# One constant added by VectorE, one batch's x on one queue, and three pauses changed in an attention-plus-experts kernel

## The chip, the cores and the metric

The kernel runs on one core of a Trainium2 chip. A core has TensorE (PE in the profile; its weight loads are shown as PEld), VectorE (DVE), ScalarE (ACT), GpSimd (POOL) and SyncE (SP). Each takes its own instructions in order, and they wait for one another through semaphores. SP, ACT and POOL can issue DMAs; a DMA waits in the issuing engine's order like any other instruction. The metric is the device time of one execution in microseconds, and the median of several executions is compared. Times inside a profile count from the start of the profiled span.

## What is computed

Two stages, all in float32. First an attention with a product feature map, for 4 batches, 4 heads, 1088 rows of 32 numbers:

```python
def phi(x):
    a = np.einsum('rd,bhsd->bhsr', S1, x)
    b = np.einsum('rd,bhsd->bhsr', S2, x)
    return np.einsum('bhsi,bhsj->bhsij', a, b).reshape(*x.shape[:-1], r * r)   # r = 8
q_p, k_p = (phi(q), phi(k))
kv = np.einsum('bhsf,bhsd->bhfd', k_p, v)
z = np.sum(k_p, axis=2)
num = np.einsum('bhsf,bhfd->bhsd', q_p, kv)
den = np.einsum('bhsf,bhf->bhs', q_p, z)[..., None] + 1e-06
return num / den
```

Its result, with the heads side by side, is x of 4352 rows by 128. Then a layer of 8 experts whose weights come from 8 rounds of Sinkhorn scaling:

```python
logits = x @ w_gate
logits = logits - logits.max()
P = np.exp(logits)                         # 4352 x 8
for _ in range(8):
    P /= P.sum(1, keepdims=True) + 1e-09
    P /= P.sum(0, keepdims=True) + 1e-09
    P *= N / E
for e in range(E):
    h = np.maximum(x @ w1[e], 0.0)         # 1024 wide
    out += P[:, e:e + 1] * (h @ w2[e])
```

## The kernel before

**The stages.** x is kept transposed in SBUF as `xT` (128 features by 4352 rows). Batch 0 is made by a path of its own (`query_products`, `multiply`, `fractions`, `divide`). Batches 1 to 3 go through `attention(b)`. Then `routing()` makes the logits, runs the Sinkhorn rounds and writes the expert weights P to DRAM (`pT`). Expert work, the large part of PE's products, starts early on rows of x that exist already, without weights (the first eight entries of `groups`, all for experts 0 and 1), and goes on with weighted x (`xe`) once P is there, from about 185 us on. The experts' second products use Strassen-like schemes: `two`/`seven` replace eight block products by seven, `four`/`twenty` do so on two levels; the sums that these need are made by VectorE (line 943 before 190 us, line 990 after).

**What sets the order.** The order on PE, DVE and ACT is the program's own, within `manual_schedule`. Expert work is a generator, `steps()`. Each of its steps issues one pair of first products (`first`, line 926), their move out of PSUM by ACT (line 930), sums on DVE that are due, and second products (`second`, line 1111) of eight steps before. `attention` and `routing` are generators too: they issue their own instructions and then yield a number, and `fill(n)` issues expert steps worth about that number before they go on. One step is worth 0.87 with the 416-row tiles that are in use around the logits. `fill` carries what it owes or has overdrawn into the next pause:

```python
    def fill(n):
        owed[0] += n
        while owed[0] > 0.25:
            owed[0] -= next(work)
```

So a `yield` sets how much expert work stands between two steps of attention or routing, on PE, DVE and ACT at once. Combining sums of a finished group (lines 750 and 753) wait in two lists, `soon` and `later`, and are issued one at a time by the steps.

**Banks.** PSUM has eight banks. Four of them (`bank()`, tiles named `a`) serve in turn for everything that is not the expert layer's long accumulation: the first products of each step, the outputs of `tops`, the three blocks of logits, and the column sums of routing. A bank can be taken again when whoever reads it has been issued, and the writer then waits until that reader is done. The other four (tiles `s`) hold the second products.

**One batch of attention.** `keys_sums` makes kv and z of a batch, `keys_kept` puts them into `kvs`, whose column D holds z. The queries come in three parts of 96 columns in each quarter (`third`). For part c, `times(b, c)` makes the products of the feature map on DVE; `tops(b, c)` multiplies them on PE by `kvs` into one bank (12 products, line 474), which gives numerators and, in column D, denominators; two more products of `ones` with the constant `eps` (1e-6 / 128 everywhere, line 478) add 1e-6 to the denominators in the same accumulation. `over(b, c)` then takes the reciprocal (line 487), multiplies (line 489) and transposes (line 493) on DVE into the tile `xt`.

**From xt to xT.** `take_over(b, lo, hi, queue)` carries columns lo to hi of `xt` to `xT`: one DMA writes them to a buffer `xd` in DRAM (line 498), four DMAs read them back in another arrangement (line 500). The reads wait for the write to land. For batches 1 and 2 all 288 columns (`W9`) go at once on POOL's queue. Batch 3 goes in two pieces: columns 0 to 192 on POOL's queue after `over(3, 1)`, and 192 to 288 on SP's queue after `over(3, 2)`.

**Logits and routing.** `logits(c)` makes a block of logits for the four batches side by side, batch 3 last, in 32-column tiles (line 508); each block takes one of the four banks `a`. `logits_turned` transposes each block on DVE (line 517) and so frees its bank. Then come the maximum (lines 593 to 600), the exponential on ACT, and the eight rounds: row sums, reciprocal, product and partial column sums on DVE (lines 608 to 614), the column sums on PE (line 618), and reciprocal and product on DVE (lines 621 and 624). At the end SP writes `pT` (line 630).

Of the kernel before, what the change touches and what calls it, by code (L numbers as in the profile page):

```python
# [10 lines left out]
F32 = mybir.dt.float32  # L11
# [39 lines left out]
def kernel(  # L51
# [12 lines left out]
    nc = tc.nc  # L64
    P = nc.NUM_PARTITIONS
    B, H, S, D = q.shape
# [77 lines left out]
    for i in range(2):  # L144
        kvs.append(consts.tile([P, 2, 2, D + 1], F32, name=f"kvs{i}"))
        nc.gpsimd.memset(kvs[i], 0.0)

    eps = consts.tile([P, 3, H], F32, name="eps")
    nc.gpsimd.memset(eps, 1e-6 / P)

    v_slots = []
    for i in range(2):
# [314 lines left out]
    def tops(b, c):  # L467

        pn = bank()[:, 0:3 * H * (D + 1)].rearrange("p (t h d) -> p t h d", t=3, h=H)
        ph = third(phs[b % 2], c)  # L470
        for t in range(3):
            for i in range(2):
                for s in range(2):
                    nc.tensor.matmul(pn[64 * s:64 * (s + 1), t, 2 * i:2 * i + 2].rearrange("p h d -> p (h d)"),  # L474
                                     ph[:, i, s, 64 * t:64 * (t + 1)], kvs[b % 2][:, i].rearrange("p h d -> p (h d)"),
                                     start=(t == 0 and i == 0), stop=False, tile_position=(0, 64 * s))
        for s in range(2):
            nc.tensor.matmul(pn[64 * s:64 * (s + 1), :, :, D], ones[:, 0:64], eps, start=False, stop=True,
                             tile_position=(0, 64 * s))
        queries[b, c] = pn  # L480

    turned = {}
# [1 line left out]
    def over(b, c):  # L484
        pn = queries.pop((b, c))
        rc = wk.tile([P, 16], F32, tag="rc", name="rc")[:, 0:12].rearrange("p (t h) -> p t h", h=H)
        nc.vector.reciprocal(rc, pn[:, :, :, D])
        xs = wk.tile([P, 512], F32, tag="rd", name="rd")[:, 0:384].rearrange("p (h t d) -> p h t d", h=H, t=3)
        nc.vector.tensor_tensor(xs.rearrange("p h t d -> p t h d"), pn[:, :, :, 0:D],
                                rc.unsqueeze(3).to_broadcast([P, 3, H, D]), op=Alu.mult)  # L490
        if c == 0:
            turned[b] = wk.tile([P, H, W9], F32, tag="xt", name="xt", bufs=1)
        nc.vector.transpose(out=turned[b][:, :, 96 * c:96 * (c + 1)].rearrange("p h (t s) -> p h t s", t=3), in_=xs)
# [25 lines left out]
    def attention(b):  # L519


        follows = b + 1 < B
        keys_sums(b)
        times(b, 0)
        yield 2.2 if b == 1 else 2
        keys_kept(b)
        times(b, 1)
        tops(b, 0)
        if b == 1:
            transpose_q(2)  # L530
        yield 1.4
        times(b, 2)
        over(b, 0)
        tops(b, 1)
        if b == 1:
            queries_ab(2)
            repeat_a(2)
        if follows:
            repeat_b(b + 1)
        yield 1.4  # L540
        over(b, 1)
        if b + 1 == B:
            take_over(b, 0, 192, nc.gpsimd)
        yield 1.4
        tops(b, 2)
        if follows:
            transpose_k(b + 1)
        if b + 2 < B:
            load_k(b + 2)
            load_v(b + 2)  # L550
        yield 1.4
        over(b, 2)
        if b + 1 < B:
            take_over(b, 0, W9, nc.gpsimd)
        else:
            take_over(b, 192, W9, nc.sync)
        if follows:
            yield 0.7
            keys_ab(b + 1)
            yield 0.7  # L560
            if b == 1:
                transpose_q(3)
            keys_products(b + 1, 0)
            yield 1.4
            keys_products(b + 1, 1)
            if b == 1:
                queries_ab(3)
                repeat_a(3)
            yield 1.4
            keys_products(b + 1, 2)  # L570
            yield 1.4
# [10 lines left out]

    def routing():

        yield 5
        for c in range(len(chunks)):
            logits(c)
        yield 1
        for c in range(len(chunks)):
            logits_turned()  # L590
        lg = lgp[:, :, 0:E]
        mx = sk.tile([P, 1], F32, tag="mx", name="mx")
        nc.vector.tensor_reduce(out=mx, in_=lg, axis=AX.XY, op=Alu.max)
        yield 3
        pm = bank()[:, 0:P]
        for s in range(2):
            nc.tensor.matmul(pm[64 * s:64 * (s + 1)], mx.to_broadcast([P, 64]), ident, start=True, stop=True,
                             tile_position=(0, 64 * s))
        nc.vector.reduce_max(mx, pm, axis=AX.X)
        nc.vector.tensor_scalar(mx, mx, -1.0, 64 * math.log(2.0), op0=Alu.mult, op1=Alu.add)  # L600
        pw = p2s[0]
        nc.scalar.activation(out=pw[:, :, 0:E], in_=lg, func=Act.Exp, bias=mx[:, 0:1])

        step = 1.5 * 2.0 ** (23 - 149 + 64)
        nc.vector.tensor_scalar(pw[:, :, 0:E], pw[:, :, 0:E], step, step, op0=Alu.add, op1=Alu.subtract)
        for it in range(ITERS):
            rs = sk.tile([P, SA], F32, tag="rs", name="rs")
            nc.vector.reduce_sum(rs, pw, axis=AX.X)  # L608
            nc.vector.reciprocal(rs, rs)
            p1 = p1s[it % 2]  # L610
            nc.vector.scalar_tensor_tensor(p1[:, 0:SA], rs.unsqueeze(2).to_broadcast([P, SA, E]), UP,
                                           pw[:, :, 0:E], op0=Alu.mult, op1=Alu.mult)
            cs = sk.tile([P, E], F32, tag="cs", name="cs")
            nc.vector.reduce_sum(cs, p1.rearrange("p g e -> p e g"), axis=AX.X)  # L614
            yield 4.25
            pc = bank()[:, 0:E]
            for s in range(2):
                nc.tensor.matmul(pc[64 * s:64 * (s + 1)], ones[:, 0:64], cs, start=True, stop=True,
                                 tile_position=(0, 64 * s))
            cr = sk.tile([P, E], F32, tag="cr", name="cr")  # L620
            nc.vector.reciprocal(cr, pc)
            last = it == ITERS - 1
            pw = lgp if last else p2s[(it + 1) % 2]
            nc.vector.scalar_tensor_tensor(pw[:, :, 0:E], cr.unsqueeze(1).to_broadcast([P, SA, E]),
                                           float(N) / E * (1.0 if last else UP), p1[:, 0:SA],
                                           op0=Alu.mult, op1=Alu.mult)

        nc.vector.transpose(out=lgT.rearrange("p a s -> p (a s)"), in_=lgp.rearrange("p a e -> p (a e)"))
        for b in (1, 0, 2, 3):
            nc.sync.dma_start(out=pT[:, b * S:(b + 1) * S],  # L630
                                                  in_=lgT[32 * b:32 * b + E].rearrange("p a s -> p (a s)"))
# [653 lines left out]
```

## Time and profile before

| | |
|---|---|
| median of 4 runs | 920.72 us (920.26 to 921.01) |
| the profiled execution | 920.52 us |
| its span | 918.7 us |
| busy: PE, DVE, ACT, POOL | 911.7, 688.5, 421.2, 213.2 us |
| granted TensorE clock | 1.00 |
| products with `ones` and `eps` (L478) | 36 records, 35.6 to 97.8 us |
| products of `tops` (L474) | 216 records, 34.9 to 97.7 us |
| logits (L508) | 24 records, 107.0 to 108.6 us |
| DMA reads of batch 3's last piece on SP | issued 102.7 to 104.0 us, 1.9 us to landing |

A row of the timeline gives the start in us, the busy time in us, the engine, the source line, the operation, what it writes and reads, the number of records that were merged, and in brackets how long the engine sat idle before and what released it. A float32 product leaves two records. Records of PE overlap, because a product's record lasts until its last result is out while the next has begun; where PE is the subject, the distance of two starts is the time that a product costs. The chain that ended last follows the work back from the last instruction; an engine's share of it says how much of the span was spent waiting for that engine.

### The profile page before, as it was taken

Reading aid. Unit: us, or ns where it says so; the run is one execution under the profiler, and the core shown is the slowest. Engines: PE = TensorE matmul, PEld = TensorE weight load, DVE = VectorE, ACT = ScalarE, POOL = GpSimd, SP = SyncE. Lnnn points to the kernel's source line nnn. Section 1 sums busy time; section 2 is a strip of 40 time slices with the busy share of each in tenths; the row PEclk is TensorE's granted clock in tenths of the full one; section 3 lists DMA queues with packets and bytes.
Section 4 is the critical chain, followed back from the end, with each engine's and each line's share of the span. In section 5 each row is a group of like instructions: output and inputs, shape, how many; then the busy total and the mean of one; then the engine's idle time right before and its main releaser. Section 6 shows DMA issues by size and latency. Waiting matters only on the chain.

```text
span 918.7 us, 18917 instructions
## 1 busy us (share of the span) xinstructions
PE 911.7 (99%) x7450; PEld 601.5 (65%) x7450; DVE 688.5 (75%) x1173; ACT 421.2 (46%) x915; POOL 213.2 (23%) x220
## 2 busy tenths in 40 slices
PE   9999999999999999999999999999999999999997
PEld 6877544466666666666666666666666666668665
DVE  7678699888877798756985666956567986668665
ACT  3355465554444454444544444544445444446443
POOL 5121100175545422200210011110100353221120
PEclk9999999999999999999999999999999999999999
DMA  9994100213554535534364343463335556452650
GB/s 250 301 280 165 54 1 1 70 64 124 157 152 132 176 129 163 176 110 148 114 181 139 114 146 109 128 194 123 136 116 168 153 149 195 158 169 93 177 151 13
DMA packets 91305, 128.15 MB, mean 139 GB/s; under 512 B 25392, under 2 KB 69504, under 8 KB 86480
## 3 DMA queue, kind: packets, MB, share of 16 engines
q1 hardware_dynamic: 88384, 121.42, 42.3%
q0 software_dynamic: 1600, 5.36, 2.0%
q8 instruction: 58, 0.95, 0.4%
q10 hardware_dynamic: 1232, 0.16, 0.1%
q14 instruction: 31, 0.25, 0.1%
HBM read 107.88 MB, written 19.05 MB: 138 GB/s over the span
## 4 chain that ended last, share of the span: by engine, by line
PE 97%; DVE 1%; DMA 1%; issue 0%; ACT 0%; SPq 0%; DVEq 0%
PE a L926 57%; PE s L1111 37%; PE a L352 1%; PE a L474 1%; DMA kx<-in_k_dram 1%; PE a L319 0%; DVE hb L943 0%; PE s L381 0%; PE a L438 0%; PE s L404 0%; PE a L508 0%; PE a L387 0%; PE a L404 0%; DVE cs L614 0%; DVE rs L608 0%
## 5 line engine op out<-in xcount | busy, mean ns | idle before, releaser
L926 PE MATMUL a<-xe,w 128*64 128x256 f32 (+1 forms) x2560 | 692.0, 470 | 0.0
L926 PEld LDWEIGHTS a<-xe,w 128*64 128x64 f32 x2560 | 320.6, 137 | 112.6 <-issue 1.6
L1111 PE MATMUL s<-hb,ws 128*64 128x256 f32 (+3 forms) x1312 | 331.6, 395 | 0.2 <-DVE hb L943 0.2
L1111 PE MATMUL s<-hx,ws 128*64 128x256 f32 x1280 | 306.3, 379 | 0.0
L930 ACT ACTIVATE hb<-a 128x256 f32<-128x256 f32 (+4 forms) x408 | 195.0, 480 | 242.2 <-PE a L926 210.2
L930 ACT ACTIVATE hx<-a 128x256 f32<-128x256 f32 (+1 forms) x360 | 167.0, 464 | 213.4 <-PE a L926 193.0
L990 DVE TENSOR_TENSOR hb<-hb 128x512 f32<-128x512 f32 (+1 forms) x204 | 140.6, 699 | 98.3 <-ACT hb L930 94.2
L1111 PEld LDWEIGHTS s<-hb,ws 128*64 128x64 f32 x1312 | 158.5, 137 | 70.1 <-issue 14.1
L990 DVE TENSOR_TENSOR hx<-hx 128x512 f32<-128x512 f32 (+1 forms) x204 | 155.4, 772 | 59.8 <-ACT hx L930 54.4
L690 POOL TENSOR_TENSOR xe<-xT,xe 128x768 f32<-128x768 f32 (+2 forms) x41 | 84.6, 2064 | 479.6 <-DMA xe<-pT 371.8
L1111 PEld LDWEIGHTS s<-hx,ws 128*64 128x64 f32 x1280 | 154.6, 137 | 57.3
L1111 PE MATMUL s<-hb,w 128*64 128x256 f32 (+3 forms) x536 | 134.7, 408 | 0.0
L926 PE MATMUL a<-xT,w 128*64 128x416 f32 (+3 forms) x512 | 120.5, 462 | 0.0
L1111 PE MATMUL s<-hx,w 128*64 128x256 f32 x384 | 95.6, 379 | 0.0
L1111 PEld LDWEIGHTS s<-hb,w 128*64 128x64 f32 x536 | 61.1, 137 | 22.9 <-issue 6.9
L943 DVE TENSOR_TENSOR hb<-hb 128x416 f32<-128x416 f32 (+7 forms) x84 | 60.3, 718 | 19.4 <-ACT hb L930 15.0
L926 PEld LDWEIGHTS a<-xT,w 128*64 128x64 f32 x512 | 50.7, 137 | 23.8 <-issue 15.1
L242 POOL TENSOR_TENSOR ws<-w 128x256 f32<-128x256 f32 (+1 forms) x70 | 62.1, 920 | 6.3 <-DMA w<-in_moe_w_dram 6.3
L943 DVE TENSOR_TENSOR hx<-hx 128x256 f32<-128x256 f32 (+1 forms) x65 | 39.0, 604 | 23.6 <-ACT hx L930 22.5
L1111 PEld LDWEIGHTS s<-hx,w 128*64 128x64 f32 x384 | 46.2, 137 | 11.6 <-DVE hx L943 0.3
L990 DVE TENSOR_TENSOR pqg<-hb 128x512 f32<-128x512 f32 x68 | 44.2, 690 | 0.0
L990 DVE TENSOR_TENSOR pqg<-hx 128x512 f32<-128x512 f32 x68 | 34.7, 549 | 0.0
(184 smaller groups left out, 486.5 us busy)
## 6 DMA issues: line engine op xcount, KB each, us to landing
w<-in_moe_w_dram SPq DMA_DIRECT2D x82, 512.0 KB, 5.6
ws<-ws SPq DMA_DIRECT2D x34, 1024.0 KB, 5.0
xe<-pT SPq DMA_DIRECT2D x34, 384.0 KB, 3.9
ws<-ws SPq DMA_DIRECT2D x12, 512.0 KB, 4.0
ph<-qa SPq DMA_DIRECT2D x12, 288.0 KB, 5.2
rb<-qb SPq DMA_DIRECT2D x3, 1152.0 KB, 7.6
pb<-pT SPq DMA_DIRECT2D x6, 384.0 KB, 7.6
kx<-in_k_dram SPq DMA_DIRECT2D x4, 544.0 KB, 5.1
```

The source lines that it names most:

```text
L242: tc.keep_in_program_order(nc.gpsimd.tensor_tensor(ws[:, c:c + len(ns)], blocks(x), blocks(y), op=Alu.subtract if off else Alu.add))
L352: nc.tensor.matmul(pv[64 * s:64 * (s + 1), i], kp[0:n, H * t + h].rearrange("p i j -> p (i j)"), vx[0:n, slots[h], t, :], start=(t == 0 an ...
L474: nc.tensor.matmul(pn[64 * s:64 * (s + 1), t, 2 * i:2 * i + 2].rearrange("p h d -> p (h d)"), ph[:, i, s, 64 * t:64 * (t + 1)], kvs[b % 2] ...
L690: tc.keep_in_program_order(nc.gpsimd.tensor_tensor(out, x, pb, op=Alu.mult))
L926: nc.tensor.matmul(ph[sl], loaded_w[j][0][:, P * f + H2 * s:P * f + H2 * (s + 1)], sources[j][:, lo:hi], start=True, stop=True, tile_posit ...
L930: nc.scalar.activation(out=out, in_=ph, func=Act.Relu)
L943: nc.vector.tensor_tensor(out, a, b, op=Alu.subtract)
L990: nc.vector.tensor_tensor(out if not isinstance(out, tuple) else places(*out), places(*a), places(*b) if isinstance(b, tuple) else b, op=A ...
L1111: nc.tensor.matmul(sums[g][i][H2 * s:H2 * (s + 1), n * place:n * (place + 1)], w, x, start=c == 1, stop=c == per, tile_position=(0, H2 * s))
```

## The change

The constant `eps` and the products with it go; `tops` ends its accumulation with its own last product. `over` adds 1e-6 to the denominators on DVE before the reciprocal. The first piece of batch 3 goes to SP's queue instead of POOL's, which puts it ahead of the second piece on the same queue. In `attention`, the pause between `tops(b, 2)` and `over(b, 2)` is 0.6 instead of 1.4 for the last batch. In `routing`, the pause ahead of the logits is 6 instead of 5.

```diff
-    eps = consts.tile([P, 3, H], F32, name="eps")
-    nc.gpsimd.memset(eps, 1e-6 / P)
-
@@ def tops(b, c):
                     nc.tensor.matmul(pn[64 * s:64 * (s + 1), t, 2 * i:2 * i + 2].rearrange("p h d -> p (h d)"),
                                      ph[:, i, s, 64 * t:64 * (t + 1)], kvs[b % 2][:, i].rearrange("p h d -> p (h d)"),
-                                     start=(t == 0 and i == 0), stop=False, tile_position=(0, 64 * s))
-        for s in range(2):
-            nc.tensor.matmul(pn[64 * s:64 * (s + 1), :, :, D], ones[:, 0:64], eps, start=False, stop=True,
-                             tile_position=(0, 64 * s))
+                                     start=(t == 0 and i == 0), stop=(t == 2 and i == 1), tile_position=(0, 64 * s))
         queries[b, c] = pn
@@ def over(b, c):
-        nc.vector.reciprocal(rc, pn[:, :, :, D])
+        nc.vector.tensor_scalar_add(rc, pn[:, :, :, D], 1e-6)
+        nc.vector.reciprocal(rc, rc)
@@ def attention(b):
         over(b, 1)
         if b + 1 == B:
-            take_over(b, 0, 192, nc.gpsimd)
+            take_over(b, 0, 192, nc.sync)
         yield 1.4
         tops(b, 2)
...
-        yield 1.4
+        yield 1.4 if follows else 0.6
         over(b, 2)
@@ def routing():
-        yield 5
+        yield 6
         for c in range(len(chunks)):
             logits(c)
         yield 1
```

## The prediction

> **What bounds the kernel now.** I read the page's busy shares and the chain that ended last first, then the timelines of TensorE (PE) around the six edits, then the timelines of the queues (SP, POOL), VectorE (DVE) and ScalarE (ACT) beside them.
>
> ```profile
> PE 911.7 (99%) x7450; PEld 601.5 (65%) x7450; DVE 688.5 (75%) x1173; ACT 421.2 (46%) x915; POOL 213.2 (23%) x220
> ...
> PE 97%; DVE 1%; DMA 1%; issue 0%; ACT 0%; SPq 0%; DVEq 0%
> ```
>
> PE is busy 911.7 of 918.7 us and 97% of the chain. So a change counts by what PE no longer executes and by the waits PE gets or loses; the other engines count only where PE waits for them. All edits act before 200 us; behind that PE meets the same work in the same order.
>
> ```profile
> 37.54 0.90 PE L474 MATMUL a<-kvs,ph 128*64 128x66 f32 x24
> 38.24 0.27 PE L478 MATMUL a<-eps,ones 128*64 128x12 f32 x4
> 38.33 0.56 PE L438 MATMUL a<-qT,wdq 128*64 128x192 f32 x4
> ```
>
> Read starts, not durations, since matmuls overlap: the removed products hold PE from 38.24 to 38.33, 0.09 us.
>
> ```profile
> 95.65 0.73 POOL L498 DMA_DIRECT2D xd<-xt  x1 [12.11 <-DVE xt L493]
> 99.20 2.19 POOL L500 DMA_DIRECT2D xT<-xd  x4 [2.82 <-DMA xd<-xt]
> ```
> ```profile
> 99.47 0.57 SPq L498 DMA_DIRECT2D xd<-xt  x1
> 102.71 1.74 SPq L500 DMA_DIRECT2D xT<-xd  x4
> ```
> ```profile
> 107.01 2.04 PE L508 MATMUL a<-xT,wg 128*32 128x512 f32 x24
> 108.98 0.92 PE L926 MATMUL a<-xT,w 128*64 128x416 f32 x4
> 109.72 0.87 PE L1111 MATMUL s<-hb,w 128*64 128x416 f32 x4
> 110.42 0.87 PE L926 MATMUL a<-xT,w 128*64 128x416 f32 x4
> ```
>
> Batch 3's x reaches xT by two write-and-read-back trips, which overlap because two queues issue them. The last of SP's four reads starts at 104.0 and lands 1.9 us later, at 105.9; the logits (L508) start at 107.01, 1.1 us behind it. So this transfer is hidden, by 1.1 us and no more.
>
> **The change, part by part.**
>
> *Products of ones (L478).* Nine `tops` lose 0.09 us each on PE: -0.8 us, six ninths of it by 87 us, all by 98 us. Bounds: 0 where PE waits right behind, 0.9 at 0.10 us each as the chain counts them. The memset of `eps` runs on POOL in the first microseconds, off the chain: 0.
>
> *Addition on DVE.* Nine additions of 128x12; nearest row: the same operation at L417 takes 0.17 us, and neighbours on DVE start 0.03 us after one another's end, so 0.2 us each (0.17 to 0.25). Behind each stand `over`'s own product and transpose and the next sums for PE. DVE works without a pause from 64.5 to 84.8 us. There the first of the two sums of the row at 69.50 is over at 69.9 and PE uses it at 70.84; that of the row at 74.24 is over at 74.6 and used at 75.57: 0.9 us of cover. One addition lies ahead of the first and two ahead of the second since DVE's last pause, and PE comes 0.2 to 0.3 us sooner: at most 0.7 of the 0.9 goes. I take 0; the upper end, all nine in PE's way, is 1.8.
>
> *Batch 3 on SP.* Nine instructions stay what they are, but SP works in order: write of 192 columns, wait for its landing, four reads, then the write of the last 96, wait, four reads. The diff's words and the order part here: the last third's write, which SP issues at 99.47 now, stands behind five new DMAs. DVE:
>
> ```profile
> 94.78 0.58 DVE L493 STREAM_TRANSPOSE xt<-rd 128x384 f32<-128x384 f32 x1
> ...
> 98.87 0.58 DVE L493 STREAM_TRANSPOSE xt<-rd 128x384 f32<-128x384 f32 x1
> ```
>
> The first two thirds are ready at 95.36; DVE's chain starts 0.5 us earlier (six `tops`) and carries two additions: 95.3. Write until reads may issue: SP's row for half the bytes takes 102.71 - 99.47 = 3.24, POOL's for the same bytes 99.20 - 95.65 = 3.55, POOL's other two trips, of half as many bytes again, 4.04 and 5.26:
>
> ```profile
> 47.08 0.59 POOL L498 DMA_DIRECT2D xd<-xt  x1 [4.51 <-DVE xt L493]
> ...
> 52.34 2.20 POOL L500 DMA_DIRECT2D xT<-xd  x4 [2.55 <-DMA xd<-xt]
> ...
> 77.32 0.59 POOL L498 DMA_DIRECT2D xd<-xt  x1 [12.52 <-DVE xt L493]
> 81.36 2.19 POOL L500 DMA_DIRECT2D xT<-xd  x4 [3.44 <-DMA xd<-xt]
> ```
>
> I take 3.55 (same bytes): 98.85. Four reads issue in 1.74: SP is free at 100.6, though the last third is ready at 99.6. Its trip is SP's own row: 3.24 to 103.85, last read 1.3 later, landing 1.9 later: **107.05 in place of 105.9**. PE, 0.8 us ahead, would start the logits at 106.2, and the fourth logits product waits for that landing: it starts at 107.15 where it now starts at 107.03. So the 0.8 us are spent here, and 0.1 more: +0.95 us, bounds 0.4 (write at 3.24 and half the additions' delay) to 3.5 (5.26, then 4.04). Behind the waiting product on PE stand all the other logits and expert products; SP's next DMA after them issues at 165.4, so nothing on SP is late. POOL, which loses its five DMAs, next works at 181.0.
>
> The Trainium skill, "DMA: Bandwidth & Descriptors", section "Issuing engines are not separate DMA queues", says that issuing from several engines saves only the sequencer's issue time. The rows above show that issue time (1.74 us), and it is what the edit gives up. The same page's "Specifications" puts the first byte at about 1 us from POOL and 0.6 from SP; by that the first write would be 0.4 us quicker and the sum 0.4 lower, which no row here shows.
>
> *The pauses (0.6 for 1.4, 6 for 5).* In the built programs PE's order is the same up to and through the logits: the sum of the pauses grows by 0.2 units, less than a step, and no expert work comes ahead of them. What moves is behind: one more step stands between the logits and their transposes (L517), and two of the eight column sums (L618, the fourth and seventh) stand one step later. Both have a price.
>
> Four PSUM banks serve `first`, logits and column sums in turn. The logits hold three until L517 has read them. Before, one step follows on the fourth bank; in the changed program three in a row take that bank, each waiting until ACT has emptied it.
>
> ```profile
> 110.00 0.52 ACT L930 ACTIVATE hb<-a 128x416 f32<-128x416 f32 x1 [1.36 <-PE a L926]
> 110.64 0.51 ACT L766 COPY m<-s 128x416 f32<-128x416 f32 x1
> 111.40 0.52 ACT L930 ACTIVATE hb<-a 128x416 f32<-128x416 f32 x1 [0.25 <-PE a L926]
> ```
>
> A step of 108.98 is emptied at 110.52; the next may start at 110.57, not 110.42: 0.15; the second at the pace of 1.40 loses 1.59 - 1.40 = 0.19. Sum +0.35 (0 to 1.35, the latter if a copy of 0.5 us stands ahead of ACT twice). L517 moves behind the sum of L753 that waits for the copy at 110.64; it is then over at 113.4, in time for the maximum at 115.3.
>
> ```profile
> 145.75 1.21 DVE L943 TENSOR_TENSOR hb<-hb 128x416 f32<-128x416 f32 x2
> ...
> 166.25 1.14 DVE L943 TENSOR_TENSOR hb<-hb 128x384 f32<-128x384 f32 x2
> ```
>
> In routing PE waits three times for sums that stand behind a Sinkhorn iteration on DVE: 0.20 us at 140.53, 0.16 at 146.39, 0.34 at 166.85. The fourth iteration now comes behind the sums of 145.75: -0.16. The seventh's column sums move from 161.84 by one step of 1.3 and end at 163.4; DVE takes them at 163.57: 0 (up to +0.3, since the chain runs through DVE there). Taken: -0.15.
>
> **Sum**, against the profiled execution (920.52, span 918.7): -0.8 + 0 + 0.95 + 0.35 - 0.15 = +0.35, so 920.9. The median of the runs is 0.2 above that execution: **921.1**.
>
> **Rivals.**
> A. *The transfer stays hidden*, landing by 106.2: -0.8 + 0.35 - 0.15 = -0.6, 920.1. For: 1.1 us of cover now. Against: the five DMAs ahead on SP cost 1.2 and PE comes 0.8 sooner.
> B. *DVE becomes the bound in attention*: up to 1.8 us over the forecast, 922.9 at the end, about 921.9 with half. For: DVE's unbroken stretch. Against: 0.9 us of cover where it is least.
> C. *Slower*: SP's two trips take POOL's slower rows, 5.26 and 4.04; the landing comes at 109.6, 2.5 us later than forecast: 923.6. It passes 0.2% (1.8 us, about what a measurement of this kernel can tell from no change) once the landing is behind 108.5. For: two trips in a row on one queue, the worst rows are of this very operation. Against: those had other traffic beside them, and here there is none.
> D. *More than meant*: the transfer is hidden, no bank wait, and all three routing waits go: -0.8 - 0.7 = -1.5, 919.2; past -0.2% (918.9) only with 0.3 us that I can't place.
>
> **How the numbers follow.** Forecast 0.5, A 0.18, B 0.09 (a third of it slow), C 0.14, D 0.09 (two thirds past the bound). Faster 0.06, same 0.77, slower 0.17. The range runs from D's 919.2 to 923.2, towards C; the forecast's own is 920.1 (lower ends of its terms) to 922.5 (a copy ahead of both bank waits, and 0.45 on the seventh iteration and its stall).
>
> **What would show it.** Right: no L478 rows; SP's second write some 1.2 us later than 99.47; PE idle or a semaphore wait of about 1 us ahead of L508's fourth product; three steps after the logits about 1.6 us apart; the idle at 146.39 gone, that at 166.85 still there. Wrong: logits at 106.2 without a wait; PE waiting for DVE sums between 60 and 85 us; the logits further back in PE's order.

## The result, and the profile after

The changed kernel takes 922.02 us (median of 34 executions, 920.34 to 923.89), the kernel before 920.29 (54 executions, 919.4 to 921.28): ratio 1.0017, 95% interval 1.0013 to 1.0022. It is slower by 1.7 us, inside the 0.2% that the forecast of 921.1 called the same, but its single executions spread over 3.5 us where those of before spread over 1.9. The profiled execution took 922.71 us, with a span of 920.9.

Busy shares and the chain that ended last, of the changed kernel:

```profile
PE 912.6 (99%) x7414; PEld 600.7 (65%) x7414; DVE 685.8 (74%) x1182; ACT 421.5 (46%) x915; POOL 211.2 (23%) x214
...
PE 92%; DMA 3%; DVE 3%; issue 0%; SPq 0%; ACT 0%; DVEq 0%
```

36 matmuls fewer, 9 VectorE instructions more. (The diff changes two pauses; the title counts three.) PE had 97% of the chain and has 92%: DMA and VectorE have stepped in. Where they do, PE's timeline shows (start, duration, engine, line, operation; in brackets the idle time ahead and what ended it). The line numbers are smaller by 3 to 6 than before; L471 is `tops`, L435 `queries_ab`, L921 and L1106 the expert products, L503 the logits, L484 the product in `over`.

```profile
37.13 0.90 PE L471 MATMUL a<-kvs,ph 128*64 128x66 f32 x24
37.84 0.85 PE L435 MATMUL a<-qT,wdq 128*64 128x192 f32 x8
38.85 0.55 PE L435 MATMUL a<-qT,wdq 128*64 128x192 f32 x4 [0.16 <-DVE rd L484]
...
39.71 0.60 PE L1106 MATMUL s<-hb,w 128*64 128x256 f32 x4
40.53 0.71 PE L921 MATMUL a<-xT,w 128*64 128x288 f32 x4 [0.22 <-DVE rd L484]
...
77.36 0.92 PE L921 MATMUL a<-xT,w 128*64 128x416 f32 x4 [0.31 <-DVE rd L484]
...
107.19 1.06 PE L503 MATMUL a<-xT,wg 128*32 128x512 f32 x6
108.82 1.99 PE L503 MATMUL a<-xT,wg 128*32 128x512 f32 x18 [0.58 <-issue]
110.74 0.92 PE L921 MATMUL a<-xT,w 128*64 128x416 f32 x4
...
112.34 0.92 PE L921 MATMUL a<-xT,w 128*64 128x416 f32 x4
...
113.93 0.92 PE L921 MATMUL a<-xT,w 128*64 128x416 f32 x4
...
168.81 0.54 PE L1106 MATMUL s<-hb,ws 128*64 128x384 f32 x1 [0.18 <-DVE hb L938]
```

The products of ones are gone: L435 follows L471. But L435 now comes in two pieces, and three times PE waits for `rd`, the tile that L484 writes. PE doesn't read `rd`. It waits because L484 is the last reader of the PSUM bank that `tops` filled, and PE's next product wants that bank. VectorE's timeline at the first two of these places, and at the end of batch 3:

```profile
37.78 0.16 DVE L481 TENSOR_SCALAR rc<-a 128x12 f32<-128x12 f32 x1
37.98 0.23 DVE L482 RECIPROCAL rc<-rc 128x12 f32<-128x12 f32 x1
38.24 0.56 DVE L484 TENSOR_TENSOR rd<-a,rc 128x384 f32<-128x384 f32 x1
...
39.83 0.56 DVE L484 TENSOR_TENSOR rd<-a,rc 128x384 f32<-128x384 f32 x1
...
95.70 0.58 DVE L488 STREAM_TRANSPOSE xt<-rd 128x384 f32<-128x384 f32 x1
...
99.96 0.58 DVE L488 STREAM_TRANSPOSE xt<-rd 128x384 f32<-128x384 f32 x1
```

L484 ends at 38.80 and 40.39; PE goes on at 38.85 and 40.53. The same places before (VectorE, then PE's step at the second):

```profile
37.92 0.56 DVE L489 TENSOR_TENSOR rd<-a,rc 128x384 f32<-128x384 f32 x1
...
39.31 0.56 DVE L489 TENSOR_TENSOR rd<-a,rc 128x384 f32<-128x384 f32 x1
...
40.25 0.69 PE L926 MATMUL a<-xT,w 128*64 128x288 f32 x4
```

There the product ended at 38.48 and 39.87, and PE, which came later, did not have to wait. Each addition takes 0.16 us, or 0.20 with the gap behind it (37.78 to 37.98), as estimated, but it stands between PE's bank and its release.

Near 38.8 us the addition is not alone. Just ahead of it VectorE stood for the load of q, which it did not do before:

```profile
35.71 1.31 DVE L299 STREAM_TRANSPOSE qT<-qx 128x1088 f32<-128x1088 f32 x1 [0.32 <-DMA qx<-in_q_dram]
```

Without these 0.32 us the product would have ended at 38.48, and PE's ninth product of L435 was due at 38.51 (eight twelfths of 1.00 us behind 37.84): almost no wait. Four more profiles below, with the additions on VectorE in this order (add_alone, add_queue, add_pauses and more_cover), have such a stand, 0.20 to 0.50 us; before, queue_alone, pauses_alone and add_on_act have none. It comes ahead of the first addition, so the addition does not cause it; what does was not tried. The waits near 40.5 and 77.4 us do not rest on it. Without it and the wait that it makes, VectorE and PE would both reach the first of them about 0.3 us sooner. Ahead of the other no such load stands, and VectorE's product ends 0.89 us later than before (77.30 for 76.41), 0.6 of it for three additions.

SP's queue of the changed kernel, with the trips of batch 3's x:

```profile
96.31 0.57 SPq L493 DMA_DIRECT2D xd<-xt  x1
99.29 1.74 SPq L495 DMA_DIRECT2D xT<-xd  x4
101.12 1.64 SPq L493 DMA_DIRECT2D xd<-xt  x1
104.68 1.73 SPq L495 DMA_DIRECT2D xT<-xd  x4
```

The last third's write starts 1.65 us later than before's 99.47. Three of the four logits products of the first chunk run from 107.19; the fourth, which needs batch 3, starts at 108.82, 1.6 us late. The profile puts the last 0.58 us of this to "issue"; that it is the transfer follows from the last read, which starts at 105.98 and lands 2.8 us later, at 108.8. Its later blocks then run without the other three column groups beside them, so the lateness of the start is the price: the block ends about 1.6 us later than it would have.

The starts of equal pieces of work on PE, from both timelines, give the account:

| work | before | after | difference |
|---|---|---|---|
| L1111/L1106, ahead of all edits | 25.80 | 25.37 | -0.43 |
| L1111/L1106 ahead of 40 | 39.82 | 39.71 | -0.11 |
| the next L1111/L1106 | 40.73 | 41.04 | +0.31 |
| L1111/L1106 near 72.7 | 72.72 | 72.66 | -0.06 |
| L1111/L1106 near 78 | 77.58 | 78.10 | +0.52 |
| logits | 107.01 | 107.19 | +0.18 |
| first step behind the logits | 108.98 | 110.74 | +1.76 |
| matmul of the maximum | 115.32 | 117.48 | +2.16 |
| L1111/L1106 near 168 | 167.88 | 169.84 | +1.96 |
| span | 918.7 | 920.9 | +2.2 |

The -0.43 at the top is no work of the change: the same row starts at 25.35 with the queue alone edited, and at 25.84 with the pauses alone. From there to the logits this execution loses 0.6 us where the forecast had it gain 0.8; at the logits 1.6 more; behind them 0.4, of which 0.2 come back, and 0.2 towards the end.

### The profile page after: what moved, and what is told of

Same layout as the page of the kernel before. It is cut to its first block, busy times and chain, and to the rows that moved or that the text cites. A ratio compares the mean times of both kernels' runs of the same rounds, so it can differ in the third digit from the quotient of the medians.

```text
span 920.9 us, 18857 instructions
## 1 busy us (share of the span) xinstructions
PE 912.6 (99%) x7414; PEld 600.7 (65%) x7414; DVE 685.8 (74%) x1182; ACT 421.5 (46%) x915; POOL 211.2 (23%) x214
## 4 chain that ended last, share of the span: by engine, by line
PE 92%; DMA 3%; DVE 3%; issue 0%; SPq 0%; ACT 0%; DVEq 0%
PE a L921 55%; PE s L1106 36%; DMA qx<-in_q_dram 1%; DMA kx<-in_k_dram 1%; DMA qb<-qab 1%; DVE hb L938 1%; PE a L349 1%; DMA v<-in_v_dram 1%; PE a L471 0%; PE a L503 0%; DVE rd L484 0%; DVE ph L462 0%; DVE cs L609 0%; DVE qT L299 0%; SPq L170 0%
## 5 line engine op out<-in xcount | busy, mean ns | idle before, releaser
L921 PE MATMUL a<-xe,w 128*64 128x256 f32 (+1 forms) x2560 | 692.0, 470 | 0.0
L921 PEld LDWEIGHTS a<-xe,w 128*64 128x64 f32 x2560 | 320.5, 137 | 112.6 <-issue 1.6
L1106 PE MATMUL s<-hb,ws 128*64 128x256 f32 (+3 forms) x1312 | 331.5, 395 | 0.2 <-DVE hb L938 0.2
L1106 PE MATMUL s<-hx,ws 128*64 128x256 f32 x1280 | 306.3, 379 | 0.0
L985 DVE TENSOR_TENSOR hb<-hb 128x512 f32<-128x512 f32 (+1 forms) x204 | 135.0, 671 | 102.3 <-ACT hb L925 98.5
L1106 PEld LDWEIGHTS s<-hb,ws 128*64 128x64 f32 x1312 | 158.6, 137 | 69.3 <-issue 14.5
L685 POOL TENSOR_TENSOR xe<-xT,xe 128x768 f32<-128x768 f32 (+2 forms) x41 | 86.1, 2100 | 498.9 <-DMA xe<-pT 359.2
L1106 PEld LDWEIGHTS s<-hx,ws 128*64 128x64 f32 x1280 | 154.5, 137 | 57.3
L1106 PE MATMUL s<-hb,w 128*64 128x256 f32 (+3 forms) x536 | 134.7, 408 | 0.0
L921 PE MATMUL a<-xT,w 128*64 128x416 f32 (+3 forms) x512 | 120.0, 462 | 0.5 <-DVE rd L484 0.5
L1106 PE MATMUL s<-hx,w 128*64 128x256 f32 x384 | 95.7, 380 | 0.0
L1106 PEld LDWEIGHTS s<-hb,w 128*64 128x64 f32 x536 | 61.1, 137 | 22.7 <-issue 6.7
L921 PEld LDWEIGHTS a<-xT,w 128*64 128x64 f32 x512 | 50.2, 137 | 25.8 <-issue 15.1
L938 DVE TENSOR_TENSOR hx<-hx 128x256 f32<-128x256 f32 (+1 forms) x65 | 36.9, 572 | 26.4 <-ACT hx L925 25.3
L1106 PEld LDWEIGHTS s<-hx,w 128*64 128x64 f32 x384 | 46.1, 137 | 11.8 <-DVE hx L938 0.6
```

What stands on the lines that cost most here:

```text
L685: tc.keep_in_program_order(nc.gpsimd.tensor_tensor(out, x, pb, op=Alu.mult))
L921: nc.tensor.matmul(ph[sl], loaded_w[j][0][:, P * f + H2 * s:P * f + H2 * (s + 1)], sources[j][:, lo:hi], start=True, stop=True, tile_posit ...
L938: nc.vector.tensor_tensor(out, a, b, op=Alu.subtract)
L985: nc.vector.tensor_tensor(out if not isinstance(out, tuple) else places(*out), places(*a), places(*b) if isinstance(b, tuple) else b, op=A ...
L1106: nc.tensor.matmul(sums[g][i][H2 * s:H2 * (s + 1), n * place:n * (place + 1)], w, x, start=c == 1, stop=c == per, tile_position=(0, H2 * s))
```

## The experiments

Medians and ratios to the kernel before, run on the same chip (before: 920.37, 920.51 and 920.23 us in the three groups):

| kernel | us, lowest to highest | ratio, 95% interval |
|---|---|---|
| add_alone | 920.61, 919.26 to 922.19 | 1.0001, 0.9992 to 1.0010 |
| queue_alone | 920.53, 919.53 to 921.01 | 1.0002, 0.9993 to 1.0010 |
| pauses_alone | 920.35, 920.13 to 920.88 | 1.0001, 0.9993 to 1.0010 |
| add_on_act | 920.01, 919.38 to 921.11 | 0.9996, 0.9987 to 1.0005 |
| add_queue | 922.29, 921.08 to 923.03 | 1.0019, 1.0010 to 1.0028 |
| add_pauses | 922.10, 919.94 to 923.74 | 1.0019, 1.0009 to 1.0029 |
| add_moved_product | 941.97, 940.6 to 945.49 | 1.0244, 1.0224 to 1.0263 |
| act_moved_product | 942.30, 940.23 to 943.02 | 1.0239, 1.0225 to 1.0253 |
| more_cover | 920.68, 919.19 to 923.51 | 1.0006, 0.9998 to 1.0015 |
| add_earlier_over | 922.40, 922.2 to 923.27 | 1.0024, 1.0015 to 1.0033 |
| act_earlier_over | 921.55, 919.84 to 922.53 | 1.0008, 0.9999 to 1.0017 |
| act_earlier_more_cover | 921.25, 919.78 to 924.05 | 1.0012, 1.0003 to 1.0022 |

The ratio is taken over the executions and is not quite that of the two medians. An interval is 0.8 us to either side, so the medians alone part only the larger effects; the waits in the profiles have to carry the rest.

### The three parts, one at a time, and the addition on another engine

**add_alone**

```diff
-        nc.tensor.matmul(..., ones[:, 0:64], eps, start=False, stop=True, ...)   # both, and eps
-        nc.vector.reciprocal(rc, pn[:, :, :, D])
+        nc.vector.tensor_scalar_add(rc, pn[:, :, :, D], 1e-6)
+        nc.vector.reciprocal(rc, rc)
```

> Only the addition on VectorE in place of the products of ones; queue and pauses as before. Theory (banks): the nine products leave PE (-0.8 us), but each addition puts off the product of `over` that frees the PSUM bank, and PE waits for that bank (idle put down to DVE, tile rd) near 38.8, 40.5 and 77.4 us, 0.3 to 0.6 us each, 0.7 to 1.3 us in all; batch 3's transfer stays hidden. Time -0.1 to +0.5 us against before. Rival (the forecast's term of 0 for the additions): no such waits, -0.8 us.

PE's timeline of add_alone:

```profile
38.65 0.55 PE L435 MATMUL a<-qT,wdq 128*64 128x192 f32 x4 [0.30 <-DVE rd L484]
...
40.34 0.71 PE L921 MATMUL a<-xT,w 128*64 128x288 f32 x4 [0.22 <-DVE rd L484]
...
77.16 0.92 PE L921 MATMUL a<-xT,w 128*64 128x416 f32 x4 [0.31 <-DVE rd L484]
...
106.99 1.06 PE L503 MATMUL a<-xT,wg 128*32 128x512 f32 x6
108.71 1.99 PE L503 MATMUL a<-xT,wg 128*32 128x512 f32 x18 [0.67 <-DMA xT<-xd]
```

The three waits for `rd` are here with the additions alone (queue_alone, below, whose PE is as early, has none). So is what I had not expected: the wait for batch 3's x at the logits, 1.7 us in this execution, although POOL's queue still takes the first piece. The eleven executions fall into two groups, six from 919.26 to 920.61 and five from 921.61 to 922.19; the profiled one, 922.19, is the slowest of all. The median of 920.61 lies where it was expected, but says little about either group.

**queue_alone** and **pauses_alone**

```diff
-            take_over(b, 0, 192, nc.gpsimd)
+            take_over(b, 0, 192, nc.sync)
```

> Only batch 3's first piece moved to SP's queue; products of ones and pauses as before. Theory: x ready at 95.36 as before, then SP's own legs as the changed kernel's profile has them (2.98 to the reads, 1.83 for the reads, 3.56 to the next reads, 1.3 to the last read) put the last read at 105.1 and its last landing 1.9 to 2.7 us later, 107.0 to 107.8; PE needs it at 107.03: a wait of 0 to 0.8 us ahead of the fourth logits product, +0 to +0.8 us, and more spread between executions than before. Rival (the queue is hidden; the changed kernel's wait comes from VectorE being late): no wait, within 0.2 us of before.

```diff
-        yield 1.4                          # ahead of the last over
+        yield 1.4 if follows else 0.6
...
-        yield 5                            # ahead of the logits
+        yield 6
```

> Only the two pauses changed (0.6 for 1.4, 6 for 5). Theory: two waits for the one free bank behind the logits, 0.15 and 0.19 us, and the idle of 0.16 us near 146.4 gone: +0.2 us (0 to 0.5). Rival (the pauses are worth nothing, or gain): 0 to -0.2 us.

SP's queue and PE's logits in queue_alone (timeline):

```profile
95.05 0.57 SPq L498 DMA_DIRECT2D xd<-xt  x1
99.02 1.74 SPq L500 DMA_DIRECT2D xT<-xd  x4
100.85 0.55 SPq L498 DMA_DIRECT2D xd<-xt  x1
103.36 1.73 SPq L500 DMA_DIRECT2D xT<-xd  x4
...
106.68 2.04 PE L508 MATMUL a<-xT,wg 128*32 128x512 f32 x24
```

All 24 logits products run in one piece of 2.04 us, as before: the whole of batch 3 on one queue is hidden when nothing else is changed. The rival for this run holds, in this profile and in the median (+0.16 us). Neither this kernel nor pauses_alone has a wait for `rd`. In pauses_alone the first three steps behind the logits start at 108.95, 110.54 and 112.14, 1.59 and 1.60 apart where before has 1.44 and 1.40: the two waits for the single bank, 0.35 us together. The idle near 146 is gone (146.25, 146.60 and 146.95 in step, where before jumps from 145.88 to 146.39). The net, 0.1 us, cannot be told from none in the median.

**add_on_act**

```diff
-        nc.vector.reciprocal(rc, pn[:, :, :, D])
+        nc.scalar.add(rc, pn[:, :, :, D], 1e-6)      # products of ones and eps gone
+        nc.vector.reciprocal(rc, rc)
```

> The products of ones replaced by an addition on ScalarE (ACT) instead of VectorE; queue and pauses as before. VectorE then executes what it did before. Theory (banks): no wait on DVE's rd between 34 and 80 us, all of the 0.8 us is kept: -0.8 us. Rival 1 (PE loses the 0.8 us anyway, at whatever it waits for next): 0, with waits in the same places as in add_alone. Rival 2 (nine instructions of about 0.2 us delay ACT's emptying of PE's banks): above -0.4 us, with PE waits put down to ACT between 34 and 100 us.

The waits near 38.8, 40.5 and 77.4 us are not in its profile, which ties the last two to the additions on VectorE (VectorE did not stand for the load of q here either). But one new wait is, at 67.59 us (waits of PE's weight loads between 60 and 75 us: engine, line, what it waited for, total, times, longest):

```profile
PEld a L921 <- DVE rd L484: 0.6, 1, 0.6
```

By the two timelines PE is 1.02 us ahead of before two steps earlier (64.63 for 65.65), 0.83 at the row just ahead (66.81 for 67.64) and 0.48 at the wait's end (67.59 for 68.07); VectorE's product ends at 67.54. So part of what PE wins is given back at the next bank, even where VectorE has nothing more to do. The median is 0.36 us under before and the interval holds both 0 and the expected -0.8; "keeps the whole" is not shown, and neither is a gain.

### What the three parts do together

**add_queue** (the changed kernel with the old pauses) and **add_pauses** (the changed kernel with POOL's queue):

```diff
-        yield 1.4 if follows else 0.6      # add_queue: back to 1.4, and 6 back to 5
-            take_over(b, 0, 192, nc.sync)  # add_pauses: back to nc.gpsimd
```

> The changed kernel with the old pauses (addition on VectorE and SP's queue for all of batch 3). Theory (the two parts add up at the logits): x is ready about 0.9 us later against PE because of the additions, and SP then starts the last third behind its own reads, so the fourth logits product waits 1 to 2 us; with the waits for banks near 39, 40.5 and 77 us, +1.3 to +1.8 us against before. Rival (the pauses carry the loss): +0.2 us or less.

> The changed kernel with batch 3's first piece back on POOL's queue (addition on VectorE and new pauses). Theory: the last third's write starts about 0.7 us earlier than in the changed kernel, but still 0.9 us later than before, and the fourth logits product waits 0 to 1.5 us depending on how long the write's leg takes; with the two bank waits behind the logits, +0.2 to +1.0 us against before, and between 0.7 and 1.3 us under the changed kernel. Rival (the queue is worth nothing): as the changed kernel, +1.7 us.

Both lose what the changed kernel loses, 1.8 and 1.6 us by their medians. For add_queue that is as expected, for add_pauses it is not: taking the queue edit back gains nothing. By the medians, though, the addition alone is at 1.0001 and either of the other two edits on top of it at 1.0019, while each of these alone is at 1.0001 or 1.0002. So by the medians the loss belongs to the addition in combination with another edit (the intervals of 1.0001 and 1.0019 only just touch); by itself the addition was seen to wait at the logits in one execution, its slowest. What the kernels with the addition on VectorE share there is read best from one number, the time from the end of VectorE's last transpose of batch 3 (the last third is then ready to be written) to the start of the logits on PE, the cover of that transfer:

| kernel | last transpose ends | logits start | cover | SP's last write to its first read | last read landed, behind the transpose | lateness of the fourth product |
|---|---|---|---|---|---|---|
| before | 99.45 | 107.01 | 7.56 | 3.24 | 6.5 | 0 |
| pauses_alone | 99.42 | 106.98 | 7.56 | 2.66 | 6.0 | 0 |
| queue_alone | 99.11 | 106.68 | 7.57 | 2.51 | 7.5 | 0 |
| add_on_act | 99.25 | 106.29 | 7.04 | 3.76 | 7.0 | 0 |
| add_alone | 100.35 | 106.99 | 6.64 | 4.52 | 8.3 | 1.7 |
| changed kernel | 100.54 | 107.19 | 6.65 | 3.56 | 8.2 | 1.6 |
| add_queue | 101.51 | 108.15 | 6.64 | 3.45 | 7.6 | 1.1 |
| add_pauses | 100.90 | 107.54 | 6.64 | 4.63 | 8.4 | 1.8 |

(The lateness is the start of the fourth product less the start of the logits; where the timeline has the block as one group, it is what the group takes over 2.04. The landing is the start of SP's last read and its time to landing.) The cover is the same to 0.01 us for the three kernels without a change to the products, and again for the four with the addition on VectorE: 0.92 us less. The parts can be read from VectorE's last wait ahead of the transpose (for ACT; 87.57 before, 88.10 in the changed kernel): from there PE takes 19.44 and 19.09 us to the logits, VectorE 11.88 and 12.44 to the end of the transpose. So 0.35 goes with the products (PE comes sooner) and 0.56 with three additions (VectorE comes later).

But the cover is only a part of the lateness. The transfer itself differs: the last read landed 6.0 to 7.5 us behind the transpose in the hidden rows and 7.6 to 8.4 in the late ones. With a transfer like before's, 6.5 us, a cover of 6.64 would have hidden it too; and the transfers of the late rows, to the fourth product 7.7 to 8.5 us, would have been 0.2 to 0.9 late at 7.56 as well. The lost cover thus accounts for 0.92 us of each lateness, the longer transfer for the rest. In the changed kernel its write starts 0.58 us behind the transpose, behind SP's own reads, and its last read lands 2.8 us after its start, for 1.9 before. Whether one of the edits lengthens the transfer, or these single profiles met long ones, is open.

### More cover

**more_cover** is the changed kernel with 0.6 undone:

```diff
-        yield 1.4 if follows else 0.6
+        yield 1.4
```

> The changed kernel with the pause of 1.4 put back ahead of the last `over` (0.6 undone, 6 kept). In the built program one whole step more of expert products (1.40 us) then stands ahead of the logits, and the three steps on one bank behind them are gone. Theory (the loss at the logits is lost cover): x has 1.4 us more until PE needs it, the wait ahead of the fourth logits product goes from 0.7-1.6 us to 0-0.3, the two bank waits behind the logits go; the waits for banks near 39, 40.5 and 77 us stay: 0 to +0.6 us against before, 1.1 to 1.7 us under the changed kernel, and less spread. Rival (the transfer itself is slowed by the queue, or the loss is elsewhere): +1.3 us or more against before.

Timeline of more_cover, PE:

```profile
40.28 0.71 PE L921 MATMUL a<-xT,w 128*64 128x288 f32 x4 [0.22 <-DVE rd L484]
...
77.11 0.92 PE L921 MATMUL a<-xT,w 128*64 128x416 f32 x4 [0.32 <-DVE rd L484]
...
108.34 2.04 PE L503 MATMUL a<-xT,wg 128*32 128x512 f32 x24
110.31 0.92 PE L921 MATMUL a<-xT,w 128*64 128x416 f32 x4
...
281.10 1.08 PE L921 MATMUL a<-xe,w 128*64 128x512 f32 x4 [0.49 <-POOL xe L685]
```

With 1.4 us of expert products more ahead of the logits the cover is 8.04 us and there is no wait. In this profile that proves little: its last read landed 6.4 us behind the transpose, which 6.64 would have hidden too. The next step behind the logits, at 111.76, is 1.45 behind the first, so the bank waits there are gone. Two of the three waits in attention stay. The median falls to 920.68 us, 1.3 under the changed kernel's (the intervals of the two ratios overlap a little). That was the expected size, and it speaks against the rival that the queue itself is the loss. The spread did not fall as expected (919.19 to 923.51), and the profiled execution, the second slowest at 922.08, has new waits: SP's write of the routing's result starts at 172.87 (before 172.15), a product of POOL with that result (L685) at 238.46 (before 235.87), and PE waits for two such products, 0.49 us at 281.10 and 0.51 at 300.77. Most of that lag arises on POOL behind the routing, so that the longer pause causes it is not shown.

### Freeing the banks sooner

**add_moved_product** and **act_moved_product** were meant to free the banks 0.9 us sooner by moving one product of VectorE:

```diff
-        times(b, 2)                        # was ahead of over(b, 0)
         over(b, 0)
...
         over(b, 1)
+        times(b, 2)
```

> As add_alone (addition on VectorE, queue and pauses as before), with one more edit: VectorE's product of the last third's features (`times(b, 2)`, 0.9 us) moved from ahead of `over(b, 0)` to behind `over(b, 1)`. The additions stay, but the banks come free 0.9 us sooner. Theory (banks): the waits for DVE's rd near 38.8 and 40.5 us vanish, that near 77.4 us stays (0.3 to 0.6); batch 3's first two thirds are ready sooner; -0.5 to 0 us against before. Rival (the loss comes from the additions' load on VectorE as a whole, not from where the banks come free): as add_alone, +0.2 us with waits of the same size.

> As add_on_act (addition on ScalarE, queue and pauses as before), with `times(b, 2)` moved behind `over(b, 1)`. Theory (banks): the wait of 0.6 us for DVE's rd near 67.6 us, where PE gave back what it had gained, vanishes too; all of the 0.8 us is kept at the logits: -0.8 us against before. Rival (PE is held by another wait as soon as this one goes): -0.4 us or less, as add_on_act.

The load of the next batch's factors (`repeat_b`) writes the tile that this product reads, and it now stood ahead of it: the product took the next batch's factors, so these two kernels compute something else, and `tops` waited for that load:

```profile
PE a L471 <- DVE ph L462: 19.4, 2, 17.0
```

(PE's waits of add_moved_product between 30 and 110 us.) Their 20 us say nothing about banks. In the next three the load moves along.

**add_earlier_over**, **act_earlier_over** and **act_earlier_more_cover**

```diff
-        times(b, 2)
         over(b, 0)
...
-        if follows:
-            repeat_b(b + 1)
         yield 1.4
         over(b, 1)
+        times(b, 2)
+        if follows:
+            repeat_b(b + 1)
```

(on add_alone; on add_on_act; on add_on_act with the pause of 6.)

> As add_alone (addition on VectorE, queue and pauses as before), with VectorE's product of the last third's features (`times(b, 2)`, 0.9 us) moved from ahead of `over(b, 0)` to behind `over(b, 1)`, and the load of the next batch's factors (`repeat_b`) moved with it. The additions stay, but the banks come free 0.9 us sooner. Theory (banks): the waits for DVE's rd near 38.8 and 40.5 us vanish, that near 77.4 us stays (0.3 to 0.6); the last third of batch 3 is not sooner, so a wait of 0 to 1.7 us ahead of the fourth logits product stays: -0.6 to +0.8 us against before. Rival (the loss in attention comes from the additions' load on VectorE as a whole): waits of the same size as in add_alone.

> As add_on_act (addition on ScalarE, queue and pauses as before), with `times(b, 2)` and `repeat_b` moved behind `over(b, 1)`. Theory (banks): the wait of 0.6 us for DVE's rd near 67.6 us, where PE gave back what it had gained, vanishes; PE is 0.8 us ahead at the logits, with 0.5 us less cover than before, so most of the executions keep the whole: -0.9 to -0.4 us against before. Rival (PE is held by another wait as soon as this one goes): as add_on_act, -0.4 us.

> As act_earlier_over, with the routing's pause of 6 for 5 (that of 1.4 ahead of the last `over` as before), so that one whole step more stands ahead of the logits. Theory (cover): never a wait ahead of the fourth logits product, the whole 0.8 us is kept in every execution, and the spread is that of before or less: -0.9 to -0.6 us against before; a routing wait may grow, since the routing starts 1.4 us later against PE (0 to +0.4). Rival (the cover was enough already, and the later routing costs): slower than act_earlier_over by 0.2 us or more.

PE's timeline of add_earlier_over:

```profile
37.71 1.17 PE L435 MATMUL a<-qT,wdq 128*64 128x192 f32 x12
38.68 0.68 PE L921 MATMUL a<-xT,w 128*64 128x288 f32 x4
...
39.60 0.68 PE L921 MATMUL a<-xT,w 128*64 128x288 f32 x4
...
40.52 0.68 PE L921 MATMUL a<-xT,w 128*64 128x288 f32 x4
...
72.01 0.92 PE L471 MATMUL a<-kvs,ph 128*64 128x66 f32 x24 [1.16 <-DVE ph L462]
...
107.15 1.06 PE L503 MATMUL a<-xT,wg 128*32 128x512 f32 x6
109.01 1.99 PE L503 MATMUL a<-xT,wg 128*32 128x512 f32 x18 [0.80 <-DMA xT<-xd]
```

The additions are all still there, and no wait for `rd` is left between 30 and 100 us. L435 runs in one piece and the steps follow one another 0.92 apart. The wait near 40.5 is the clear case: VectorE's second product ends at 39.00 (38.44 and 0.56), and PE's step starts at 39.60 without a wait; behind the moved product, which took 0.84 us of VectorE's order there (36.94 to 37.78 in the changed kernel), it would have been too late. So this wait is one for a bank, not for VectorE's load as a whole. The other two are less clear: near 38.8 VectorE did not stand for the load of q in this execution, and the wait near 77.4, which was expected to stay, goes because PE comes later. As a repair it fails: the moved product is now late itself, and `tops` of batch 2's last third waits 1.16 us for it, more than was won (from the row near 25 us to the logits it takes 82.09 us, add_alone 81.69). The cover stays 6.64 us and the fourth product is 1.8 late, so the kernel is at 922.40.

The two on ScalarE miss their expectations outright: by their ratios 0.7 and 1.1 us over before instead of 0.4 to 0.9 under. Each has the same wait at L471 (1.17 and 0.9 us), and act_earlier_more_cover one for a bank besides (0.53 us at L435), in an execution in which VectorE had stood 0.94 us for the load of q just before: such a load moves the bank's release as an addition does. act_earlier_over has a cover of 6.98 us and met a slow transfer (8.8 us, lateness 1.8). act_earlier_more_cover has 8.36 us and met one of 8.7: late by only 0.4, so the cover does what it should. Its executions spread from 919.78 to 924.05, which the wait at the logits, 0.4 in the slowest, does not explain. In that one, the profiled, PE waits three times more for POOL's products (L685), as in more_cover: 0.51 us each at 302.32 and 322.00, and ahead of them (its timeline, PE):

```profile
244.60 1.08 PE L921 MATMUL a<-xe,w 128*64 128x512 f32 x4 [0.87 <-POOL xe L685]
```

No kernel tried is shown to beat the one before.

## Why the prediction was right or wrong

The direction, slower by less than 0.2%, and the range held; the sum did not. It had +0.35 us where 1.7 were measured. The larger part of the miss is the products with the additions: the sum had -0.8 for them, add_alone's ratio gives +0.1 and its median +0.24. The rest is, in the profile, a transfer that took longer than forecast.

- **Products of ones, -0.8.** The removal works between waits: from 40.73 to 72.72 the difference falls by 0.37 us while four `tops` lose their products, 0.09 each. But little of the 0.8 reaches the logits even with VectorE left alone: in add_on_act they start 0.72 us sooner than before, and PE was 0.67 ahead at its row near 25 us already (25.13 for 25.80). Where PE comes sooner, the next bank is not free; the bound "0 where PE waits right behind" was nearer.
- **Addition on DVE, "I take 0".** This is the step that failed. I sought the cover in the sums that PE uses from VectorE, 0.9 us at the least, and these were indeed never waited for. What ended last was another thing that stands behind the addition: the PSUM bank that `over`'s product hands back. (One sign that the forecast named for being wrong, PE waiting for VectorE between 60 and 85 us, came, at 77.36, but for a bank and not for sums.) There the margin was 0.5 us at 38.48 (PE's ninth product of L438 was due at 39.0: the twelve take 1.00 from 38.33) and 0.38 at 39.87 (PE went on at 40.25). An addition or two, PE's own gain, and in this execution PE's earlier start and 0.32 us that VectorE stood for the load of q use that up. From the rows, PE is late by 0.34 us at 38.85 (by the same pace the ninth was due at 38.51), 0.39 at 40.53 (due 0.43 after 39.71, as before), and from the keys' products (75.75; before, 75.81) to L921 at 77.36 (76.88) it takes 0.54 more: 1.27 us at the three places that PE's rows put down to `rd` (the idle times in their brackets, 0.16, 0.22 and 0.31 us, are shorter, since a record lasts until its last result is out). About 0.3 us of it, near 38.8, is the load of q as much as the addition. Rival B, which had VectorE binding in attention at 921.9 with half of its price, named the right engine and the wrong reason.
- **Batch 3 on SP, +0.95.** Link by link the forecast of these ten instructions (it says nine) was near: 95.3, 98.85, 100.6, 103.85 against 96.28, 99.29, 101.12, 104.68. All are later, the first by 1.0, the bank waits that VectorE's chain inherits; the first leg took 2.98 us for 3.55, the second 3.56 for 3.24. The last read then landed late, 2.8 us behind its issue (104.68 + 1.3), where the forecast allowed 1.9: the fourth product started at 108.82 for a forecast 107.15, behind the 108.5 that rival C named as its turning point. The cover was forecast well: logits at 106.2 and the last third ready at 99.6 make 6.6 us, and 6.65 were measured, both ends about 1.0 us later. Of the slack of 1.1 us before, the addition and the products took 0.9; what turned the rest into a wait of 1.6 is the transfer, 8.28 us from the transpose to the fourth product for a forecast 7.55. The forecast put this to the queue. The queue alone costs nothing that shows, and putting it back with the pauses changed gains nothing; but on top of the addition the queue edit and the pauses each go with 1.5 to 1.7 us more in the median than add_alone, and why is open.
- **Pauses, +0.35 and -0.15.** Right: 1.60 and 1.59 us from step to step behind the logits in the changed kernel, the idle at 146.39 gone, the one before L1111 at 166.85 still there at 168.81, PE's order up to the logits unchanged. Alone they are worth nothing measurable. What they gave away is larger: 1.4 in place of 0.6 puts a whole step ahead of the logits, and more_cover's median is 1.3 us lower with it.

Of the loss, then, the bank waits net of the products make about 0.6 us and the wait for batch 3 the most, 1.6 in the profiled execution. That execution is 0.7 us slower than the median; I put this down to how long the transfer took in it, but only single profiles were taken, and that the two groups of executions in add_alone are a fast and a slow transfer was not shown.

The Trainium skill, "DMA: Bandwidth & Descriptors", section "Issuing engines are not separate DMA queues", says that DMAs of several engines interleave on the same DMA engines and that only issue time is saved by spreading them. The runs agree: SP, alone, starts the last third's write 0.6 to 1.7 us behind the last transpose (its own four reads of 1.74 us stand ahead) and not at once, but the leg from write to first read is then 2.5 to 3.6 us in four profiles, against 2.7 to 4.6 in the eight in which POOL's reads were in flight beside it. The estimate from its "Specifications" had the first write on SP 0.4 us quicker than on POOL; the runs show about 0.3: 2.99 us to the first read at the median of four profiles, 3.30 at that of eight.

## What to carry to other kernels

An instruction added between a matmul and the last reader of its PSUM bank can cost what the next user of that bank waits (0.39 us at 40.53 here), so look for the cover there as well as at the results that other engines read. A transfer hidden by a small margin is shared property: work removed from the engine that consumes it and work added to the engine that feeds it both spend that margin, and an edit that costs nothing alone may cost in company. Compute such a cover as one difference (ready time to use time) and compare it over kernels; it repeated to 0.01 us where the medians were uncertain by 0.8. Then set the transfer's own length beside it, over several kernels: here that varied more (6.0 to 8.7 us from transpose to landing) than the cover lost.

## What was not expected of the hardware

The same DMA of 192 KB, written by SP, took from 2.48 us (more_cover) to 4.63 (add_pauses) until its first read could issue, in profiles of kernels that differ little there. In the changed kernel and in add_queue the write's issue on SP lasted 1.64 and 1.54 us, where it lasts 0.55 to 0.57 in the other kernels. What sets either was not tried.
